# A two-layer hedgehog-attention and gated-MLP kernel whose planner follows a written list of decisions up to the second MLP block

## The chip, the cores and the metric

The kernel runs on one core of a Trainium2 chip. A core has five engines that work side by side, each through its own list of instructions in order: TensorE (PE in the profile, with its weight loads as PEld), VectorE (DVE), ScalarE (ACT), GpSimd (POOL) and SyncE (SP), which here issues nearly all transfers. They wait for each other through semaphores. The metric is device time in microseconds (us): the median of 4 runs was 1060.17 us (1059.71 to 1062.53).

## The reference

```python
def _A_ref(x, wqkv, w_phi, wo):           # S=2048, D=576, H=32 heads of Dh=18
    q, k, v = split of x @ wqkv into heads
    pq, pk = q @ w_phi, k @ w_phi         # per head, 18x18
    phi_q = concat(softmax(pq), softmax(-pq))
    phi_k = concat(softmax(pk), softmax(-pk))
    kv = phi_k^T v;  z = sum of phi_k over the sequence
    return ((phi_q kv) / (phi_q z + 1e-6)) @ wo
def _B_ref(x, w_gate, w_up, w_down):      # F=4608
    return ((x @ w_gate) * (x @ w_up)) @ w_down

x = A_x
x = x + _A_ref(_layernorm(x), A_wqkv, A_w_phi, A_wo)
x = x + _B_ref(_layernorm(x), B_w_gate, B_w_up, B_w_down)
x = x + _A_ref(_layernorm(x), A_wqkv, A_w_phi, A_wo)
x = x + _B_ref(_layernorm(x), B_w_gate, B_w_up, B_w_down)
```

The definitions are shortened here to what is computed. All inputs are bf16; the same weights serve both layers. The input B_x is not used.

## The kernel before

**Stages.** The 2048 rows are 16 tiles of 128, taken in pairs; a pair is also a block of the MLP (8 blocks per layer). All weights but the down weights stay in SBUF. First the raw query and key weights are multiplied by w_phi (threads fusek0 to fusek4 and fuseq0 to fuseq4, t_fuse1: five transposes at L1125, a copy, and two halves of three matmuls each at L1139 with a copy behind each). At the same time TensorE forms Gram products of the raw weights (flag, L999; m2, L981 and L984), from which a bound on the exponents follows. VectorE reduces it to one number in SBUF (L1002, L1008, L1012, with a count on TensorE at L1010), and every engine then loads that number and branches (emit_two, the "mark"). The branch taken here is the fast one, which needs no maxima in the softmax. What stands ahead of the mark in an engine's list runs before the branch.

**Layer 1's attention.** For each pair lnA1 normalises the rows (statistics L1179 to L1193 on VectorE, reciprocal root L1200 and L1202 on ScalarE, product L1212) and puts them in transposed form: by TensorE (L1223) for the first tiles, by a transposing transfer (L1230) for the others. For each tile v1 makes the values and ain1 the keys (both L1256), four exponentials on ScalarE (L1377), one sum on VectorE (L1444), a reciprocal, two multiplications on GpSimd (L1459; on VectorE for tiles 14 and 15); for every second tile TensorE then adds the key-value products of both tiles (L1498). When all are in, VectorE masks the sums (bar1, L1589), and aout1 makes numerators (L1646), a division, a transpose and the output projection of a tile. pq1 projects the queries of tiles 2 to 15 ahead (L1256). The projections are done as two interleaved streams of 64-row matmuls, one in each half of the array; transposes, fused weights, key-value products, numerators and the down projection use its full height.

**The MLP.** For each block gate and up products (glu, gu_quad, L1788, 64-row form, nine groups of four parts) go to hT by ScalarE (L1835) and VectorE (L1837), then dn makes 36 steps of the down product (L1862, L1864) from weights that SP loads slot by slot (wd1, L1763). The attention of later tiles and of layer 2 is woven into the blocks.

**Who sets the order.** Nothing is reordered on the chip. When the program is built, a planner (Sched.run) goes over some hundred threads (generators such as t_ain). Each offers its next step: a group of operations on one engine, one that may go to either of two engines ("alt"), or a transfer. The planner estimates when each could start and records the step with the smallest key

```python
key = (est - self.bias.get(int(th.prio), 0.0) - th.age - th.age0 - (self.hold if late else th.boost), -th.prio)
```

where `age0` comes from the table AGES, by the thread's name. Each engine's list is the order in which its steps were recorded. While no step is far along, `keep_warm` fills TensorE with matmuls on zeros (L957). SP's list is set in the same way: x loads and weight loads from t_load, transposes of xT, eT and oT, and the down weights.

Of the kernel before, what the change touches and what calls it, by code (L numbers as in the profile page):

```python
# [16 lines left out]


AGES = {
    "ain1_0": 64, "ain1_1": -84, "ain1_12": -99, "ain1_13": 49, "ain1_14": 167, "ain1_15": -2, "ain1_2": 26, "ain1_3": 15, "ain1_4": -23,  # L20
    "ain1_5": -128, "ain1_6": -79, "ain1_7": 168, "ain1_8": -58, "ain1_9": -129, "ain2_14": -581, "aout1_0": 4, "aout1_3": -408, "aout2_0": -253,
    "aout2_1": 5, "aout2_2": -160, "aout2_3": -342, "bar1": -1145, "bar2": -651, "bdphi": 663, "bepi0": 843, "bepi6": 1283, "bepi7": -480,
    "flag": -97, "fusek1": 416, "fusek2": 111, "fusek3": 264, "fuseq0": 11, "fuseq4": -53, "init": 108, "k2_6": -644, "k2ln0": 204, "k2ln1": 1008,
    "kv2_6": 13, "kv2_7": -60, "lnA1_0a": 466, "lnA1_0b": 209, "lnA1_1": -113, "lnA1_2": -355, "lnA1_3": 125, "lnA1_6": -93, "lnA1_7": 72,
    "lnB1_0a": 155, "lnB1_0b": -798, "lnB2_0a": -48, "lnB2_0b": 270, "m2": 114, "pq1_11": 129, "pq1_2": -581, "pq1_3": -501, "pq1_4": -398,
    "pq1_7": 408, "pq1_8": 379, "pq1_9": 735, "pq2_11": 158, "pq2_12": -146, "pq2_13": -162, "pq2_14": -2, "pq2_15": -156, "pq2_2": 116, "pq2_3": -76,
    "pq2_5": -209, "pq2_6": -46, "pq2_7": -103, "pq2_8": 448, "pq2_9": 459, "v1_0": -120, "v1_1": 18, "v1_10": -205, "v1_11": 63, "v1_12": -142,
    "v1_13": 263, "v1_2": 195, "v1_3": -176, "v1_4": 267, "v1_5": -60, "v1_6": 31, "v1_7": -90, "v1_8": 232, "v1_9": -307, "v2_14": -73,
    "v2_15": -358,
}  # L30


class Tracker:
# [282 lines left out]
class Sched:  # L316

    def __init__(self, tracker):
        self.tr = tracker
        self.free_at = {e: 800.0 for e in ENGINES}  # L320
        self.busy = {e: 0.0 for e in ENGINES}
        self.threads = []
        self.pools = {}
        self.events = set()
        self.ev_time = {}
        self.dma_free = {e: 0.0 for e in ENGINES}
        self.dma_bw = 280.0
        self.dma_lat = 2000.0
        self.log = []
        self.bias = {}  # L330
        self.pe_mode = 0
        self.fill = None
        self.warm_at = 6000.0
        self.pe_switch = 100.0
        self.lock = None
        self.open = False
        self.hold = -1500.0
        self.port = {"dve": 0.0, "pool": 0.0}
        self.alt_cost = {"dve": 1.0, "pool": 1.0, "act": 1.0}
# [82 lines left out]
    def port_time(self, eng, op, t):  # L422
        if eng == "pool":
            return max(t, self.port["dve"])
        if op.port:
            return max(t, self.port["pool"])
        return t

    def keep_warm(self, limit):

# [24 lines left out]
    def run(self):  # L455
        tr = self.tr
        while True:
            progressed = False
            again = True
            while again:  # L460
                again = False
                for th in list(self.threads):
                    while th.req is not None and th.req[0] not in ("ops", "alt", "pe2", "dma", "acq", "acqn"):
                        r = th.req
# [72 lines left out]
            self.threads = [t for t in self.threads if t.req is not None]  # L537
            if not self.threads:
                break
            best = None  # L540
            pe_est = 1e12
            for th in self.threads:
                r = th.req
                if r[0] == "alt":
                    pick = None
# [28 lines left out]
                    raise RuntimeError("scheduler deadlock: %s" % [(t.name, t.req[:2]) for t in self.threads])  # L574
                continue
            _, th, est = best
            if self.fill is not None:
                self.keep_warm(min(pe_est, est))
            r = th.alt if th.req[0] in ("alt", "pe2") else th.req
            if r[0] == "ops":  # L580
                eng = r[1]
# [108 lines left out]
class K:  # L690
    def __init__(self, nc, A_x, A_wqkv, A_w_phi, A_wo, B_w_gate, B_w_up, B_w_down, out, fast, base=None):
# [13 lines left out]
        self.wtdma = ''  # L705
        self.valt = False
        self.qalt = True
        self.sload = [['raw', 2], ['raw', 1], ['x0', 0], ['raw', 0], ['raw', 3], ['x0', 1], ['x', 1], ['raw', 4], ['x', 2], ['wv', 0], ['x', 3]]
        self.aload = []
        self.fage = 150  # L710
        self.fageq = 0.0
        self.fage2 = 600
        self.lnb = 3
        self.pes = (0, 1, 2, 3, 4, 5, 6, 7, 8, 9, 10, 11, 12, 13)
        self.early = (2, 2)
        self.pex = 2
# [1 line left out]
        self.alt = 1.2  # L718
        self.wage = 10
        self.lnage = -3  # L720
        self.lnlead = 8
        self.pol0 = 1
        self.qdeep = (1, 1)
# [7 lines left out]
        self.qcrit = False  # L731
        self.fq = 3
        self.fqs = 2
        self.fqp = 6.15 if fast else 6.5
        self.sub2pool = False
        self.rboost = 500.0
        self.prio0 = (6, 7)
# [359 lines left out]
    def t_fuse(self, which):  # L1097
# [4 lines left out]
        for kt in range(5):  # L1102
            if which == "q" and not s.fast:
                yield ("wait", ("ain", 1, s.fq + s.fqs * kt))
            yield ("go", s.t_fuse1(which, kt), s.fqp if which == "q" else 8, "fuse%s%d" % (which, kt))
            if which == "q":
                yield ("wait", ("w", which, kt))
        for kt in range(5):
            yield ("wait", ("w", which, kt))
        yield ("sig", ("w", which))  # L1110
# [399 lines left out]
    def t_ain(self, L, st_):  # L1510
# [16 lines left out]
        yield ("wait", ("v", L, st_))  # L1527
        vxs = s.vx_of[(L, st_)]
        if L == 1:
            if s.fast and st_ % 2 == 0:  # L1530
                s.sm_of[st_] = sm
                yield ("sig", ("kf1", st_))
                return
            if s.fast:
                yield ("wait", ("kf1", st_ - 1))
                sm0, vx0 = s.sm_of[st_ - 1], s.vx_of[(1, st_ - 1)]
                for bi in range(2):
                    yield ("ops", "pe", s.kv_ops(sm0, vx0, bi, s.kvb[bi], None, False) + s.kv_ops(sm, vxs, bi, s.kvb[bi], None, False))
                yield ("rel", "smx", sm0 - s.NSM)
                yield ("rel", "vxx", vx0 - s.NVX)  # L1540
                yield ("sig", ("ain", 1, st_ - 1))
            else:
                for bi in range(2):
                    yield ("ops", "pe", s.kv_ops(sm, vxs, bi, s.kvb[bi], None, False))
# [608 lines left out]
```

## Time and profile before

| What | Value |
|---|---|
| median of 4 runs | 1060.17 us |
| the profiled execution's own time | 1060.47 us |
| its span in the profile | 1058.7 us |
| TensorE busy | 1047.1 us (99%) |
| VectorE, ScalarE, GpSimd busy | 480.6, 346.7, 190.7 us |
| first key projection starts | 16.81 us |
| first gate product of block 0 / block 1 starts | 91.93 / 149.57 us |

The span is measured from the first to the last instruction of the profile; the run's time is 1.8 us longer. A timeline line has the start, the length, the engine, the kernel's line, the operation, what it writes and reads, the form and the count; in brackets stands the engine's idle time before it and who ended it. A matmul's form 64*128 uses half the rows of the array. Matmul ends are modelled, so the distance between starts says more than the length. In the table by stage each pair of numbers is an engine's busy time and its count, in the order PE, PEld, DVE, ACT, POOL, then the granted clock, the share of the transfer engines and GB/s.

### The profile page before, as it was taken

The numbers are of one execution on the slowest core, as the hardware profiler recorded it, in microseconds if no ns is written. First come the engines' busy times: TensorE is split into PE (matmuls) and PEld (weight loads), VectorE is DVE, ScalarE is ACT, GpSimd is POOL, SyncE is SP. The second block draws the span as 40 slices with busy tenths as digits, with TensorE's granted clock in tenths as the row PEclk, the third lists the DMA queues.
The fourth block names the chain that finished last, engine by engine and source line by source line (L and its number), as shares of the span: only waits on it lengthen the run. The fifth ranks groups of instructions, "written<-read, shape, count | busy, mean of one in ns | idle before, by whom it ended". The sixth has DMA issues, their size and how long they took to land.

```text
span 1058.7 us, 34326 instructions
## 1 busy us (share of the span) xinstructions
PE 1047.1 (99%) x15789; PEld 803.0 (76%) x15851; DVE 480.6 (45%) x972; ACT 346.7 (33%) x843; POOL 190.7 (18%) x204
## 2 busy tenths in 40 slices
PE   8999999999999999999999999999999999999998
PEld 6778868687786868778695786877778686868685
DVE  7875545264544435444232663534334243424131
ACT  6876314133242414225141742222313131202020
POOL 3952112030221203013110120201010101000000
PEclk9999999999999999999999999999999999999999
DMA  5595281652708164351606034545271918181704
GB/s 163 110 359 143 41 232 39 180 84 83 169 16 228 35 191 73 98 132 37 205 12 202 2 59 145 120 105 156 72 190 41 222 15 239 24 222 19 211 4 149
DMA packets 177625, 127.78 MB, mean 121 GB/s; under 512 B 96576, under 2 KB 175680, under 8 KB 176320
## 3 DMA queue, kind: packets, MB, share of 16 engines
q1 hardware_dynamic: 176864, 125.47, 45.5%
q8 instruction: 126, 2.06, 0.8%
q14 instruction: 27, 0.22, 0.1%
q10 hardware_dynamic: 608, 0.02, 0.0%
HBM read 100.82 MB, written 2.36 MB: 97 GB/s over the span
## 4 chain that ended last, share of the span: by engine, by line
PE 93%; DMA 3%; POOL 2%; DVE 1%; ACT 1%; issue 0%
PE ps L1788 54%; PE ps L1862 20%; PE ps L1256 11%; PE ps L1864 4%; DMA wdr<-in_B_w_down_dram 1%; PE ps L1646 1%; POOL dd_h1g L1459 1%; DMA wdx<-in_B_w_down_dram 1%; PE ps L1498 1%; PE ps L1244 0%; PE ps L1223 0%; POOL xln L1212 0%; POOL dd_w3f L1459 0%; DMA wst<-in_A_w_phi_dram 0%; ACT dd_h1g L1377 0%
## 5 line engine op out<-in xcount | busy, mean ns | idle before, releaser
L1788 PE MATMUL ps<-xT,Wu 64*128 64x256 bf16 x4608 | 581.6, 269 | 0.0
L1788 PE MATMUL ps<-xT,Wg 64*128 64x256 bf16 x4608 | 581.1, 269 | 0.0
L1788 PEld LDWEIGHTS ps<-xT,Wg 64*128 64x128 bf16 x4608 | 430.5, 94 | 30.9 <-issue 3.3
L1788 PEld LDWEIGHTS ps<-xT,Wu 64*128 64x128 bf16 x4608 | 431.7, 94 | 27.9
L1837 DVE TENSOR_TENSOR hT<-ps,hT 128x512 bf16<-128x512 f32 x288 | 199.2, 692 | 302.4 <-ACT hT L1835 302.4
L1835 ACT CAST hT<-ps 128x512 bf16<-128x512 f32 x288 | 168.5, 585 | 400.6 <-PE ps L1788 396.2
L1862 PE MATMUL ps<-wdr,hT 128*128 128x512 bf16 x922 | 238.8, 380 | 0.6 <-DMA wdr<-in_B_w_down_dram 0.3
L1864 PE MATMUL ps<-wdr,hT 128*128 128x64 bf16 x960 | 184.9, 193 | 2.3 <-issue 0.5
L1459 POOL TENSOR_TENSOR dd<-dd,ss 128x576 bf16<-128x576 bf16 x92 | 106.6, 1184 | 441.6 <-ACT ss L1455 441.6
L1862 PEld LDWEIGHTS ps<-wdr,hT 128*128 128x128 bf16 x960 | 93.8, 98 | 111.3 <-DMA wdr<-in_B_w_down_dram 1.8
L1788 PE MATMUL ps<-xT,Wr 64*128 64x256 bf16 x1152 | 165.3, 269 | 0.0
L1212 POOL TENSOR_SCALAR xln<-x_sb,nmean,rstd 128x576 bf16<-128x576 bf16 x56 | 45.4, 821 | 331.4 <-DVE nmean L1193 151.2
L1905 DVE TENSOR_TENSOR x_sb<-ps,x_sb 128x64 bf16<-128x64 f32 x32 | 7.0, 220 | 213.9 <-PE ps L1864 213.9
L1864 PEld LDWEIGHTS ps<-wdr,hT 128*128 128x128 bf16 x960 | 94.1, 98 | 0.2
L1455 ACT ACTIVATE ss<-ss 128x64 f32<-128x64 f32 x92 | 23.8, 259 | 196.2 <-DVE ss L1444 195.3
L1444 DVE TENSOR_REDUCE ss<-dd 128x64 f32<-128x1152 bf16 x48 | 63.8, 1346 | 16.6 <-ACT dd L1377 10.8
L1788 PEld LDWEIGHTS ps<-xT,Wr 64*128 64x128 bf16 x1152 | 63.1, 94 | 6.6
L1862 PE MATMUL ps<-wdx,hT 128*128 128x512 bf16 x168 | 50.4, 380 | 0.6 <-DMA wdx<-in_B_w_down_dram 0.6
L1256 PE MATMUL ps<-Wv,xT 64*128 64x288 bf16 x576 | 49.4, 283 | 0.2 <-ACT dd_h1g L1377 0.2
L1256 PE MATMUL ps<-Wk,xT 64*128 64x288 bf16 x576 | 48.4, 283 | 0.0
L1179 DVE BATCH_NORM_STATS2 st<-x_sb 128x6 f32<-128x288 bf16 x120 | 46.3, 445 | 0.8 <-DVE flag L1012 0.7
L1256 PE MATMUL ps<-Wq,xT 64*128 64x288 bf16 x576 | 40.6, 283 | 0.2
(131 smaller groups left out, 739.1 us busy)
## 6 DMA issues: line engine op xcount, KB each, us to landing
wdr<-in_B_w_down_dram SPq DMA_DIRECT2D x240, 288.0 KB, 3.5
wdx<-in_B_w_down_dram SPq DMA_DIRECT2D x48, 288.0 KB, 3.5
Wg<-in_B_w_gate_dram SPq DMA_DIRECT2D x4, 1152.0 KB, 17.0
Wu<-in_B_w_up_dram SPq DMA_DIRECT2D x4, 1152.0 KB, 18.7
out_dram<-x_sb SPq DMA_DIRECT2D x16, 144.0 KB, 2.7
x_sb<-in_A_x_dram SPq DMA_DIRECT2D x7, 288.0 KB, 3.2
Wraw<-in_A_wqkv_dram SPq DMA_DIRECT2D x5, 304.0 KB, 4.3
xT<-xln SPq DMA_TRANSPOSE x54, 2.5
```

The source lines that it names most:

```text
L1179: ops.append(Op(d_dve(288), (lambda e, j=j, h=h, src=src: e.bn_stats(st[:, sl[j], 6 * h:6 * h + 6], src)), reads=rd, writes=[("st", sl[j], ...
L1212: em = (lambda e, j=j: e.tensor_scalar(xln[:, sl[j], 0:576], x_sb[:, ss[j], :], s.nmean[:, sl[j]:sl[j] + 1], rstd[:, sl[j]:sl[j] + 1], ALU ...
L1256: out.append(Op(61, (lambda e, h=h, k=k, st=(i == 0 and k == 0), sp=(i == 1 and k == 3): e.matmul(s.ps[:, banks[h], 0:N], L[r, k, :], Wm[r ...
L1444: Op(1265, (lambda e: e.tensor_reduce(ss[:, sm, :], e4, AX.X, ALU.add)), reads=s.ddk(sm, 0) + s.ddk(sm, 1), writes=[("ss", sm)]),
L1455: yield ("ops", "act", [Op(200, (lambda e, kw=kw: e.activation(ss[:, sm, :], ss[:, sm, :], **kw)), reads=[("ss", sm)], writes=[("ss", sm)])])
L1459: yield ("alt", [(eng, [Op(dur, (lambda e, ev=ev, rb=rb: e.tensor_tensor(ev, ev, rb, ALU.mult)), reads=s.ddk(sm, br) + [("ss", sm)], write ...
L1498: ops.append(Op(d_pe(CW * n) + 3, (lambda e, k=k, c0=c0, h=h, n=n, st=(first and k == bi): e.matmul(s.ps[:, bank, c0:c0 + CW * n], phi[:, ...
L1788: out.append(Op(54.3, (lambda e, bank=bank, cs=cs, lhsT=lhsT, rhs=rhs, st=st, sp=sp: e.matmul(ps[:, bank, cs].rearrange("p (a n) -> p a n" ...
L1835: yield ("ops", "act", [Op(480, (lambda e, gb=gb, p=p: e.copy(hT[:, p, :], ps[:, gb, :])), reads=[("gu", gb)], writes=[("hT", p)] + (s.raw ...
L1837: yield ("ops", "dve", [Op(600, (lambda e, ub=ub, p=p: e.tensor_tensor(hT[:, p, :], ps[:, ub, :], hT[:, p, :], ALU.mult)), reads=[("gu", u ...
L1862: ops = [Op(d_pe(512), (lambda e: e.matmul(s.ps[:, bank, 0:512], lhsT, s.wslot(slot)[:, fi, 0:512], start=(f == 0), stop=(f == NF - 1))), ...
L1864: Op(d_pe(64) + 3, (lambda e: e.matmul(s.ps[:, z, 64 * sl:64 * sl + 64], lhsT, s.wslot(slot)[:, fi, 512:576], start=(f == 0 and (sl == 0 o ...
```

## The change

The planner gets a list, ORDER, of 980 words. A word is a thread's name, if need be with the engine it should take ("/act"). The n-th time that a name stands there is that thread's n-th step. As long as words are left (`left`), `scripted` takes, among the threads that offer a step now, the one whose step stands earliest in the list; only if none stands there the old key decides. The words reach to the last steps of the down product of block 1 of layer 1 (dn1_1). For a step that may go to two engines the named one is taken, otherwise the cheaper by the old estimate; a word like "/act" behind a step that has no such choice has no effect. Behind the list the planner goes on as before.

Besides: AGES has new numbers for threads that the list covers, and the old ones for all others; the first two raw weight blocks are loaded in the other order; `lnb` goes from 3 to 5 (from which pair on lnA1 waits for the branch); `fqp`, a priority of the fuseq threads, from 6.15 to 6.5; `fqd` and `kvg` are new parameters for the wait between fuseq threads and for which tiles share a group of key-value products.

```diff
@@ -17,17 +17,69 @@
 
 
 AGES = {
...
+ORDER = """
+init side init load init side load load init load init init/act init load/act load flag load/act bdphi fusek1/act m2 fusek1/pool flag/act
+m2/pool lnA1_0a/pool m2 fusek1/pool load fusek2 load/act flag fusek1 lnA1_0a/pool fusek3/pool lnA1_0a lnA1_0b m2 m2 lnA1_0a flag lnA1_0a
+fusek3 fusek3 lnA1_0b/dve lnA1_0b load load lnA1_0b/act lnA1_0a/dve fusek2/pool fusek3 lnA1_0b/act flag load flag fusek0 fusek1 fusek2/dve
+lnA1_0a fusek4 flag fusek0 fusek3 fusek2/pool flag fusek0 lnA1_0b fusek3 fusek2 fusek0/act fusek2 fusek4 fusek4/pool flag fuseq0/act
+init/act fusek1 fusek0 lnA1_0b fusek4/act v1_0 lnA1_1 fuseq0 init fusek4/act fuseq0/pool v1_0/act fusek0 v1_1 fusek4 lnA1_1/dve v1_0 load
+fuseq0/pool lnA1_1 ain1_0 load/pool v1_1 lnA1_1 lnA1_2 lnA1_1 lnA1_1 v1_0/pool ain1_0/act v1_1/act v1_1/act fuseq0/pool ain1_0 fuseq0 lnA1_2
+ain1_0 fuseq1 lnA1_2/dve lnA1_2 lnA1_1 ain1_0/act ain1_0/dve lnA1_1/dve ain1_1/pool lnA1_2 fuseq1 lnA1_1 lnA1_1 ain1_1 ain1_0 lnA1_1 lnA1_3
+ain1_2 lnA1_3 load/dve lnA1_2 fuseq1 ain1_1/dve ain1_1/dve v1_2 ain1_0 ain1_1 ain1_1/dve lnA1_3/pool lnA1_2 fuseq1 lnA1_3/pool ain1_2 ain1_2
+ain1_2 lnA1_2 ain1_1/act v1_2 ain1_0 fuseq1/pool ain1_0 v1_2/dve lnA1_3 ain1_2/pool fuseq1 ain1_2 ain1_3 ain1_1 lnA1_3 v1_3/pool ain1_3/pool
...
+fuseq3 ain1_6 lnA1_5/pool ain1_6 ain1_5 fuseq3 ain1_7 lnA1_4/pool ain1_5/dve v1_6/act fuseq3 v1_7/dve fuseq4 ain1_6/act ain1_7/act ain1_6
+fuseq4 ain1_7/act v1_7/act lnA1_5 ain1_7 ain1_7 ain1_6 v1_7 ain1_7 ain1_8 v1_6/pool fuseq4 v1_8 v1_7 ain1_8 fuseq4 ain1_8/act ain1_5 v1_8
+ain1_8/pool ain1_5 v1_8/pool fuseq4 v1_8 ain1_8 ain1_5 lnA1_6 ain1_9 ain1_6 ain1_7 ain1_7 lnA1_6 ain1_7/pool lnA1_5 ain1_8 fuseq4/dve pq1_2
+lnA1_6 ain1_9/act lnA1_5 lnA1_5 ain1_7 ain1_8 lnA1_6/act ain1_7 lnA1_6 lnA1_7 lnA1_7 lnA1_7/dve lnA1_6 ain1_9 lnA1_6 v1_9 ain1_9 lnA1_6/act
+pq1_2 ain1_8 ain1_8/act lnA1_7 lnA1_7 v1_9 pq1_2 v1_9/act pq1_2 ain1_10/act v1_9 lnA1_6 lnA1_6/dve load load v1_10/dve ain1_10 ain1_9/dve
...
+v1_13 aout1_0 aout1_0 aout1_0 aout1_1 ain1_13 aout1_0 load ain1_12 v1_13 ain1_14/dve v1_13 v1_14 ain1_13 ain1_14 aout1_1 aout1_1 aout1_1
+aout1_1 aout1_0 ain1_14/act ain1_15 ain1_14 ain1_13 v1_14 aout1_1/pool v1_14 ain1_15 v1_14 ain1_15 ain1_11 ain1_14/dve ain1_14 ain1_15/pool
+ain1_15 aout1_0 load aout1_1 ain1_14 ain1_15/pool v1_15 pq1_3 aout1_1 ain1_15/dve v1_15 aout1_0/dve ain1_15 pq1_3 ain1_14 v1_15 pq1_3 pq1_4
+pq1_5/pool pq1_3 aout1_1 ain1_15 v1_15 pq1_4 aout1_0/pool pq1_5 pq1_4/act ain1_15 pq1_6 ain1_14 ain1_11/act pq1_4 pq1_6 pq1_5 pq1_5/act
+pq1_6 pq1_7/pool aout1_0 ain1_13 aout1_0 pq1_6 pq1_7/pool ain1_14/act ain1_15/dve pq1_7 aout1_0 ain1_13/act ain1_15 aout1_0 aout1_1 pq1_7
+wd1/dve wd1 wd1/act pq1_9 bar1 bar1 aout1_1 aout1_2 aout1_0 aout1_1/act aout1_1 aout1_0 aout1_0 pq1_9 aout1_1 pq1_9 pq1_8/act aout1_1
+aout1_2 aout1_0 pq1_9 aout1_0 pq1_10 aout1_1 aout1_1/act aout1_0/pool aout1_0/act aout1_0 aout1_1 aout1_3 aout1_0/pool aout1_1/pool lnB1_0a
+aout1_0 aout1_1 aout1_1 aout1_1/pool lnB1_0a aout1_1/dve aout1_0 lnB1_0b/pool lnB1_0b/dve lnB1_0a aout1_3 lnB1_0b aout1_2 pq1_11 wd1/pool
+wd1 lnB1_0a aout1_1/pool lnB1_0a aout1_1 pq1_11/act pq1_8/pool wd1 aout1_2 lnB1_0a pq1_8 pq1_11/act pq1_11 aout1_2 aout1_3/pool pq1_10/dve
+pq1_12 lnB1_0b aout1_2 pq1_8 pq1_13/act pq1_10 aout1_3 lnB1_0a pq1_12 pq1_12 lnB1_0b pq1_12 aout1_3 pq1_14/pool pq1_13 pq1_14/act pq1_13
+aout1_3 pq1_10 aout1_2 pq1_15 lnB1_0b pq1_15/dve lnB1_0b pq1_14 glu glu glu glu pq1_14/act aout1_3 glu aout1_2 pq1_15 aout1_4 glu glu
+aout1_4 glu glu pq1_13 aout1_4 pq1_15/act glu glu aout1_4/act glu glu glu/pool glu glu/act aout1_4/pool glu glu glu/act glu aout1_4 aout1_2
...
+wd1 dn1_1 aout1_7 dn1_1 aout1_7 dn1_1 wd1 dn1_1 aout1_7 dn1_1 wd1 dn1_1 dn1_1 wd1 dn1_1 dn1_1 wd1 dn1_1 dn1_1 wd1 dn1_1 dn1_1 wd1 dn1_1
+dn1_1 wd1 dn1_1 dn1_1 wd1 dn1_1 dn1_1 wd1 dn1_1 dn1_1 wd1 dn1_1 dn1_1 wd1 dn1_1 dn1_1 wd1 dn1_1 dn1_1 wd1 dn1_1 dn1_1 wd1 dn1_1
+"""
...
 class Tracker:
@@ -329,6 +381,10 @@
         self.log = []
         self.bias = {}
         self.pe_mode = 0
+        self.steps = {}
+        self.seq = []
+        self.rank, self.pick = {}, {}
+        self.script(ORDER.split())
         self.fill = None
         self.warm_at = 6000.0
         self.pe_switch = 100.0
@@ -425,6 +481,54 @@
         if op.port:
             return max(t, self.port["pool"])
         return t
+
+    def script(self, words):
+        n = {}
+        for i, w in enumerate(words):
+            name, _, eng = w.partition("/")
+            k = (name, n.get(name, 0))
+            n[name] = k[1] + 1
+            self.rank[k] = i
+            if eng:
+                self.pick[k] = eng
+        self.left = len(self.rank)
+
+    def scripted(self):
+
+        best = None
+        for th in self.threads:
+            if th.req[0] in ("ops", "alt", "pe2", "dma"):
+                r_ = self.rank.get((th.name, self.steps.get(th.name, 0)))
+                if r_ is not None and (best is None or r_ < best[0]):
+                    best = (r_, th)
+        if best is None:
+            return None
+        th = best[1]
+        r = th.req
+        if r[0] == "alt":
+            pick = None
+            want = self.pick.get((th.name, self.steps.get(th.name, 0)))
+            for i_, (eng, ops) in enumerate(r[1]):
+                e_ = self.port_time(eng, ops[0], max(self.free_at[eng], self.ready(th, i_, eng, ops, False), th.t_ready))
+                f_ = (eng != want) * 1e9 * bool(want) + e_ + sum(o.dur for o in ops) * self.alt_cost[eng]
+                if pick is None or f_ < pick[0]:
+                    pick = (f_, e_, eng, ops)
+            est = pick[1]
+            th.alt = ("ops", pick[2], pick[3])
+        elif r[0] == "pe2":
+            ops = r[1 + self.pe_mode]
+            est = max(self.free_at["pe"], self.ready(th, 10 + self.pe_mode, "pe", ops, True), th.t_ready)
+            th.alt = ("ops", "pe", ops, self.pe_mode)
+        elif r[0] == "ops":
+            eng = r[1]
+            est = self.port_time(eng, r[2][0], max(self.free_at[eng], self.ready(th, 20, eng, r[2], True), th.t_ready))
+            if eng == "pe" and r[2][0].mode != self.pe_mode:
+                est += self.pe_switch
+        else:
+            est = max(self.free_at[r[9] if len(r) > 9 else "sp"], self.ready(th, 21, "sp", r, False), th.t_ready)
+        if self.fill is not None and (r[0] == "pe2" or (r[0] == "ops" and r[1] == "pe")):
+            self.keep_warm(est)
+        return (None, th, est)
     def keep_warm(self, limit):
@@ -537,9 +641,10 @@
             self.threads = [t for t in self.threads if t.req is not None]
             if not self.threads:
                 break
-            best = None
+            best = self.scripted() if self.left > 0 else None
+            told = best is not None
             pe_est = 1e12
-            for th in self.threads:
+            for th in () if told else self.threads:
                 r = th.req
                 if r[0] == "alt":
                     pick = None
@@ -574,8 +679,11 @@
                     raise RuntimeError("scheduler deadlock: %s" % [(t.name, t.req[:2]) for t in self.threads])
                 continue
             _, th, est = best
-            if self.fill is not None:
+            if self.fill is not None and not told:
                 self.keep_warm(min(pe_est, est))
+            self.left -= told
+            self.steps[th.name] = self.steps.get(th.name, 0) + 1
+            self.seq.append((th.name, len(self.log)))
             r = th.alt if th.req[0] in ("alt", "pe2") else th.req
             if r[0] == "ops":
                 eng = r[1]
@@ -705,12 +813,12 @@
         self.wtdma = ''
         self.valt = False
         self.qalt = True
-        self.sload = [['raw', 2], ['raw', 1], ['x0', 0], ['raw', 0], ['raw', 3], ['x0', 1], ['x', 1], ['raw', 4], ['x', 2], ['wv', 0], ['x', 3]]
+        self.sload = [['raw', 1], ['raw', 2], ['x0', 0], ['raw', 0], ['raw', 3], ['x0', 1], ['x', 1], ['raw', 4], ['x', 2], ['wv', 0], ['x', 3]]
         self.aload = []
         self.fage = 150
         self.fageq = 0.0
         self.fage2 = 600
-        self.lnb = 3
+        self.lnb = 5
         self.pes = (0, 1, 2, 3, 4, 5, 6, 7, 8, 9, 10, 11, 12, 13)
         self.early = (2, 2)
         self.pex = 2
@@ -718,6 +826,8 @@
         self.alt = 1.2
         self.wage = 10
         self.lnage = -3
+        self.fqd = 1
+        self.kvg = [0, 2, 4, 6, 8, 10, 12, 14]
         self.lnlead = 8
         self.pol0 = 1
         self.qdeep = (1, 1)
@@ -731,7 +841,7 @@
         self.qcrit = False
         self.fq = 3
         self.fqs = 2
-        self.fqp = 6.15 if fast else 6.5
+        self.fqp = 6.5 if fast else 6.5
         self.sub2pool = False
         self.rboost = 500.0
         self.prio0 = (6, 7)
@@ -1103,8 +1213,8 @@
             if which == "q" and not s.fast:
                 yield ("wait", ("ain", 1, s.fq + s.fqs * kt))
             yield ("go", s.t_fuse1(which, kt), s.fqp if which == "q" else 8, "fuse%s%d" % (which, kt))
-            if which == "q":
-                yield ("wait", ("w", which, kt))
+            if which == "q" and kt >= s.fqd - 1:
+                yield ("wait", ("w", which, kt - s.fqd + 1))
         for kt in range(5):
             yield ("wait", ("w", which, kt))
         yield ("sig", ("w", which))
@@ -1527,18 +1637,22 @@
         yield ("wait", ("v", L, st_))
         vxs = s.vx_of[(L, st_)]
         if L == 1:
-            if s.fast and st_ % 2 == 0:
+            g0 = max(c for c in s.kvg if c <= st_)
+            g1 = min([c for c in s.kvg if c > st_] + [NS]) - 1
+            if s.fast:
                 s.sm_of[st_] = sm
+            if s.fast and st_ < g1:
                 yield ("sig", ("kf1", st_))
                 return
             if s.fast:
-                yield ("wait", ("kf1", st_ - 1))
-                sm0, vx0 = s.sm_of[st_ - 1], s.vx_of[(1, st_ - 1)]
+                for t_ in range(g0, g1):
+                    yield ("wait", ("kf1", t_))
                 for bi in range(2):
-                    yield ("ops", "pe", s.kv_ops(sm0, vx0, bi, s.kvb[bi], None, False) + s.kv_ops(sm, vxs, bi, s.kvb[bi], None, False))
-                yield ("rel", "smx", sm0 - s.NSM)
-                yield ("rel", "vxx", vx0 - s.NVX)
-                yield ("sig", ("ain", 1, st_ - 1))
+                    yield ("ops", "pe", [o for t_ in range(g0, g1 + 1) for o in s.kv_ops(s.sm_of[t_], s.vx_of[(1, t_)], bi, s.kvb[bi], None, False)])
+                for t_ in range(g0, g1):
+                    yield ("rel", "smx", s.sm_of[t_] - s.NSM)
+                    yield ("rel", "vxx", s.vx_of[(1, t_)] - s.NVX)
+                    yield ("sig", ("ain", 1, t_))
             else:
                 for bi in range(2):
                     yield ("ops", "pe", s.kv_ops(sm, vxs, bi, s.kvb[bi], None, False))
```

## Prediction before the run

> **What bounds the kernel now.** I read the page first: busy times, then the chain that ended last.
>
> ```profile
> PE 1047.1 (99%) x15789; PEld 803.0 (76%) x15851; DVE 480.6 (45%) x972; ACT 346.7 (33%) x843; POOL 190.7 (18%) x204
> ...
> PE 93%; DMA 3%; POOL 2%; DVE 1%; ACT 1%; issue 0%
> ```
>
> TensorE is the bound; a new order only helps where TensorE stands still or pays for being asked in a bad sequence. The table by stage, for the stretch that the list rewrites, says how little standing still there is (first pair of numbers: length, then TensorE's busy time).
>
> ```profile
> 0.00:13.20 13.20, 10.32 (x132) 8.84 (x132) 7.94 (x29) 6.37 (x15) 3.99 (x17) 1.00 0.81 260
> 13.20:25.00 11.80, 11.78 (x164) 7.97 (x166) 11.27 (x30) 9.79 (x32) 4.75 (x8) 1.00 0.19 58
> 25.00:47.00 22.00, 21.58 (x338) 15.41 (x336) 19.23 (x37) 18.55 (x68) 21.57 (x21) 1.00 0.59 116
> 47.00:75.00 28.00, 27.86 (x451) 20.89 (x450) 20.85 (x28) 21.33 (x71) 20.90 (x20) 1.00 0.90 291
> 75.00:92.00 17.00, 17.00 (x236) 12.27 (x234) 10.92 (x26) 12.98 (x35) 3.39 (x3) 1.00 0.90 311
> ```
>
> Idle: 2.88 us before 13.2, 0.58 us from there to 92, where the first gate/up product starts. But "busy" contains modelled ends, so I also took the spacing of matmul starts in the timeline. First the branch on the flag:
>
> ```profile
> 10.53 0.89 DVE L1002 TENSOR_REDUCE cst<-ps 128x1 f32<-128x384 f32 x2
> ...
> 11.18 0.82 POOL L1212 TENSOR_SCALAR xln<-x_sb,nmean,rstd 128x576 bf16<-128x576 bf16 x1 [7.27 <-DVE cst L1002]
> ...
> 11.46 0.57 DVE L1008 TENSOR_SCALAR f<-cst 128x2 bf16<-128x2 f32 x1
> ...
> 12.08 0.19 PE L1010 MATMUL ps<-one,f 128*1 128x1 bf16 x2 [0.61 <-DVE f L1008]
> 12.33 0.14 DVE L1012 TENSOR_SCALAR flag<-ps 1x1 int32<-1x1 f32 x1
> ...
> 13.20 0.57 PE L1223 MATMUL ps<-ident,xln 128*128 128x128 bf16 x6 [0.93 <-DVE flag L1012]
> 13.60 0.31 PE L1139 MATMUL ps<-BDphi,WTk 128*64 128x144 bf16 x3
> ```
>
> TensorE waits 0.61 us for the comparison and 0.93 us for flag and branch: 1.54 us with nothing queued ahead of the branch. Second, the price of changing between the 64-row matmuls (two halves of the array side by side) and full-height ones:
>
> ```profile
> 17.43 0.65 PE L1256 MATMUL ps<-Wv,xT 64*128 64x288 bf16 x8
> 17.92 0.65 PE L1256 MATMUL ps<-Wk,xT 64*128 64x288 bf16 x8
> 18.50 0.32 PE L1139 MATMUL ps<-BDphi,WTq 128*128 128x108 bf16 x3
> 18.65 0.56 PE L1223 MATMUL ps<-ident,xln 128*128 128x128 bf16 x6
> ...
> 21.36 0.32 PE L1139 MATMUL ps<-BDphi,WTq 128*128 128x144 bf16 x3
> 21.61 0.79 PE L1256 MATMUL ps<-Wk,xT 64*128 64x288 bf16 x10
> ```
>
> Eight 64-row matmuls before more of the same take 17.92 - 17.43 = 0.49 us, before full-height ones 18.50 - 17.92 = 0.58; three full-height ones 0.15 before their like, 0.25 before 64-row ones. A switch costs 0.09 to 0.10 us each way, 0.19 us there and back. Third, waits inside the stretch; the largest is this one:
>
> ```profile
> 45.49 0.33 PE L1139 MATMUL ps<-BDphi,WTq 128*64 128x108 bf16 x3
> 45.76 0.35 PE L1498 MATMUL ps<-vx_h2g,dd_h1g 128*128 128x76 bf16 x5
> 46.34 0.69 PE L1498 MATMUL ps<-vx_h2g,dd_h1g 128*128 128x76 bf16 x13 [0.23 <-POOL dd_h1g L1459]
> ```
>
> Here the spacing reaches 0.43 us where 0.04 is normal: 0.39 lost. Going through all starts from 13.2 to 92 the same way (against 0.12 us for a pair of 64-row matmuls), the other losses are 0.19 at 24.65, 0.25 at 28.6, 0.17 at 28.9, 0.09 at 40.4, 0.08 at 50.5, 0.17 at 53.5, 0.19 at 58.1, 0.2 at 71.3, 0.16 at 82.1 and about 0.2 in crumbs: 2.1 us with the first. So what an order can win is about 1.5 + 2.1 us, plus switches.
>
> **The change, part by part.** *Edits that move nothing by themselves.* The pair list for the key-value products is the old pairing, and the depth of 1 for the fused query weights gives the old wait. The ages that changed all belong to threads that the list steers; those of later threads are as before. The layer norms of pairs 3 and 4 no longer wait for the branch, but the list puts their first step behind the flag's last. Raw weight blocks 1 and 2 swap places in the load queue: equal sizes (304 KB), so the landings (3.68 and 4.72 us) swap owners. Together 0; a cost needs a reader of block 2 standing first, and the list asks for block 1 first.
>
> *The start.* I laid the list's TensorE words before the flag's ninth and last step beside the timeline. Before: five weight transposes, seven of the ten key-weight halves, one layer norm transpose. New: the same five, eight halves, both layer norm transposes, most of the extra behind the matmul that counts the flag. What moves into the idle time is one transpose group (13.60 - 13.20 = 0.40 us) and one half (13.84 - 13.60 = 0.24): 0.64 us. Does the flag come later? The last Gram block can't start before its weights land (9.38; it ran at 9.89), so it can gain at most 0.5. Behind it stand the maxima (0.89), the comparison, the count, the flag; the list puts copies of about 0.45 us each (rows of the same copies at 9 to 12 us) between them, two probably on VectorE. Against that, the comparison took 0.57 us beside GpSimd's 0.82 us normalisation, and a VectorE operation of that size elsewhere 0.15 (its negated mean, 9.95). The Trainium skill (SBUF — State Buffer, Who interferes with whom) says that VectorE in its two-port modes and GpSimd hold a shared pair of ports exclusively for a whole instruction; the row agrees in kind (11.46 + 0.57 = 12.03, GpSimd's end 12.00). The list doesn't fix which engine normalises the second tile: on VectorE the 0.4 us goes. By row and rule the flag moves by -0.5 to +0.5; I take 0. Cost also: the negative one, that the weight check's first reduction now follows the 0.9 us product of mask and weights on VectorE, so its matmul stands some 0.4 us at 5.6; the Gram block that ends the chain is bound by its landing, which hides it. Sum **-0.65** (-1.2 to +0.3).
>
> *Switches.* Counting changes of form up to the last down product of block 1: 58 in the trace of before, 60 in the list. One pair more: **+0.19**. The Trainium skill (TensorEngine Tiling (Array Packing), Key Properties) says that a change of tiling mode drains the engine, and TensorE: Matmul & The Clock Gate, Single matmul latency, puts a drain near 175 ns. By that rule a pair would be 0.35 us; the measured rows give half of it, and I use them. This rule speaks against the change: nothing was won on switches.
>
> *Waits from 13.2 to 92.* The list keeps the shape: first key-value products behind tile 4, those of tiles 4 and 5 behind tile 8. GpSimd's queue ahead of the products of tiles 6 and 7 is the same 8 normalisations and 16 multiplications: 8 x 0.81 + 16 x 1.165 = 25.1 us from its start at 20.67, plus an idle 0.85, which ends at 46.3 to 46.6, the wait shown. In the list 0.6 us more TensorE work (half a query projection) stands ahead of that wait, and the ScalarE steps before GpSimd's first normalisation (its reciprocal root) follow the first key projection, which the start brings 0.6 us forward. The two roughly keep step, so this wait shrinks but stays possible. Tiles 14 and 15 get more cover: 12 half projections between the last key projection and its product (9.4 us by 0.56 each plus transposes and products), where before 6.6 us sufficed. New exposure: the second tile's transpose before block 0 is followed by only 8 matmuls (0.49 us) before the gate product reads its copy (0.49 us on VectorE, 0.69 on ScalarE, some 0.1 around): +0.15 (0 to +0.4). Of the 2.1 us I let half go, with no row that says which half: -1.1 (-2.1 to +1.0, since a new order can make as many). Sum **-0.95**.
>
> *Transfers.* The load of x pair 3 moves behind the branch on SP: issued near 13.1 it lands about 2.9 us later (as pair 4 did, 13.10 to 15.99); its first reader was at 21.9. The gate and up weights keep their place behind the last normalised tile's transposes; the last one landed at 84.40 for a reader at 91.9, so 7.5 us of slip are free. Behind six down-weight loads stand the attention transposes of tiles 2 and 3 (landed 91.5 and 97.4, read at 103.8). The output projection of tile 2 comes earlier: 8.1 us behind its numerator (4.5 + 0.5 + 56 x 0.0545), where the chain took 8.0 (103.8 to the landing at 111.81); its transpose took 4.4 us with two others near, the next 2.6, and the list issues those others later. **0** (to +0.4).
>
> *After block 1* the planner is the old one with the old ages: **0**, bounded by 1 us each way, since the few waits there depend on how the first blocks leave the queues.
>
> Sum: -0.65 + 0.19 - 0.95 = -1.4 us. Against the profiled execution's 1060.47 (span 1058.7, 1.8 around it) that is 1059.1; the median 1060.17 lies 0.3 lower, so **1058.8**.
>
> **The rivals.** *Small gain* (0.44): the sum; 1057.8 to 1062.2 is within 0.2%, 2.1 us, about what a measurement of this kernel can tell from no change. This holds too if the order does nothing: GpSimd's chain at 46 us then swallows the gain of the start, 1060.0. *Nearly all of it goes* (0.34): 1.5 at the flag and most of the 2.1, less 0.19, so about -3: 1057.2. For it: every wait named is short and has other work near; against: GpSimd's row at 25 to 47 is 98% busy, and that chain is not shortened. *Slower* (0.22): GpSimd's chain starts late. TensorE is in order, and everything queued behind the products of tiles 6 and 7 waits with them. By my sum TensorE gets there at about 45.4, so a start after 20.3 costs us for us; from 23.8 on (2.1 + 1.4 later) the kernel is measurably slower, at 24.5 it takes 1063. Before, GpSimd idled 6.5 us for exactly this start, on ScalarE's root behind a full queue; against it, the list keeps the root behind the same four exponentials.
>
> **Numbers.** Faster 0.36 (the second case and the edge of the first), within 0.2% 0.42, slower 0.22. Range 1056.4 (all waits and the flag, -3.8) to 1062.4 (GpSimd's late start and one more wait); the small gain alone: 1057.8 to 1060.4.
>
> **What would show it.** Right: TensorE has work between count and branch, the first key projection starts near 16.2 (16.81 now), gate/up starts at 90.5 (91.93) and everything from there is shifted evenly. Wrong: the flag's operation on VectorE after 12.6, GpSimd's first long run later than 20.7, a gap before the first gate product above 0.4, or spacing lost after 210 us.

## The result, and the profile after

The changed kernel takes 1059.12 us (median of 34 runs, 1057.6 to 1062.27) where the kernel before, run beside it, takes 1060.5 (55 runs, 1058.77 to 1063.45). The ratio is 0.9988, with a 95% interval of 0.9983 to 0.9994: 0.6 to 1.8 us faster, 1.3 in the middle. The forecast was 1058.8, 1.4 us below the runs of before, and "within 0.2%" as the likeliest class; both held. How the 1.3 us came about did not follow the forecast. The profiled execution took 1059.69 us (span 1057.9), 0.78 less than that of before.

The page first: busy times, then the chain that ended last.

```profile
PE 1047.6 (99%) x15791; PEld 805.7 (76%) x15853; DVE 480.0 (45%) x971; ACT 346.1 (33%) x836; POOL 193.8 (18%) x208
...
PE 96%; DMA 1%; DVE 1%; ACT 1%; issue 0%; POOL 0%
```

TensorE is the bound as before. The table by stage (length, then busy time and count of TensorE, and so on as before) answers to the five rows of the prediction:

```profile
0.00:13.20 13.20, 12.01 (x152) 10.73 (x154) 7.67 (x29) 8.20 (x18) 4.64 (x20) 1.00 0.74 238
13.20:25.00 11.80, 11.59 (x165) 8.32 (x167) 11.02 (x29) 9.85 (x34) 5.99 (x8) 1.00 0.42 103
25.00:47.00 22.00, 21.70 (x340) 15.44 (x336) 19.83 (x39) 16.72 (x59) 21.81 (x22) 1.00 0.57 102
47.00:75.00 28.00, 27.64 (x447) 20.81 (x443) 21.78 (x27) 21.99 (x71) 20.83 (x19) 1.00 0.97 293
75.00:92.00 17.00, 16.85 (x233) 12.14 (x234) 11.56 (x29) 11.34 (x30) 4.83 (x5) 1.00 0.74 294
```

Up to 13.2 us TensorE is idle for 1.19 us instead of 2.88: 1.69 less. From there to 92 us it is idle for 1.02 us instead of 0.58: 0.44 more. So the start earned, and the list behind it gave something back. VectorE's timeline at the check of the weights, and TensorE's in the same stretch, show the start:

```profile
10.09 0.89 DVE L1112 TENSOR_REDUCE cst<-ps 128x1 f32<-128x384 f32 x2 [0.55 <-PE ps L1109]
11.02 0.23 DVE L1118 TENSOR_SCALAR f<-cst 128x2 bf16<-128x2 f32 x1
...
11.55 0.14 DVE L1122 TENSOR_SCALAR flag<-ps 1x1 int32<-1x1 f32 x1
12.40 0.49 DVE L1336 COPY xT<-ps 128x640 bf16<-128x640 bf16 x1 [0.71 <-PE ps L1249]
```

```profile
8.87 0.56 PE L1333 MATMUL ps<-ident,xln 128*128 128x128 bf16 x6
9.43 0.73 PE L1109 MATMUL ps<-Wraw 128*128 128x128 bf16 x10
10.00 0.44 PE L1235 MATMUL ps<-ident,Wraw 128*128 128x128 bf16 x5
...
11.30 0.19 PE L1120 MATMUL ps<-one,f 128*1 128x1 bf16 x2
11.42 0.32 PE L1249 MATMUL ps<-BDphi,WTk 128*128 128x144 bf16 x3
11.59 0.56 PE L1333 MATMUL ps<-ident,xln 128*128 128x128 bf16 x6
12.08 0.58 PE L1249 MATMUL ps<-BDphi,WTk 128*128 128x108 bf16 x6
...
15.46 0.41 PE L1366 MATMUL ps<-Wk,xT 64*128 64x288 bf16 x3
```

TensorE no longer stands still behind the count (11.30): the second tile's transpose (11.59, 13.20 before) and two more groups run while the flag is made and read. But the chain to the flag is shorter too. The last Gram group starts at 9.43 (9.89 before) although its weights land at 9.38 in both, the comparison takes 0.23 us (0.57 before), and the flag is done at 11.69 instead of 12.47. The first key projection starts at 15.46 (16.81), the first gate product at 91.45 (91.93), block 1 at 148.92 (149.50 by the first gate product in the trace of before; the 149.57 in the table further up is 0.07 too late). Of a lead of 1.35 us at the first key projection 0.48 reaches block 0, and the span ends 0.7 earlier. The waits on TensorE that stand out between the two are these:

```profile
18.20 0.57 PE L1333 MATMUL ps<-ident,xln 128*128 128x128 bf16 x6 [0.15 <-ACT Wq L1254]
26.91 0.78 PE L1366 MATMUL ps<-Wk,xT 64*128 64x288 bf16 x9 [0.24 <-ACT dd_h1g L1487]
60.70 0.66 PE L1366 MATMUL ps<-Wq,xT 64*128 64x288 bf16 x8 [0.30 <-PE ps L1366]
```

In spacing of starts they cost 0.3, 0.4 and 0.47 us. The wait on GpSimd at 46 us, the largest of before, is gone: the same 18 products now run as one row.

```profile
45.69 0.86 PE L1608 MATMUL ps<-vx_h2g,dd_h1g 128*128 128x76 bf16 x18
```

### The profile page after: what moved, and what is told of

Its sections match the earlier page's. It is cut to its first block, busy times and chain, and to the rows that moved or that the text cites. A ratio compares the mean times of both kernels' runs of the same rounds, so it can differ in the third digit from the quotient of the medians.

```text
span 1057.9 us, 34326 instructions
## 1 busy us (share of the span) xinstructions
PE 1047.6 (99%) x15791; PEld 805.7 (76%) x15853; DVE 480.0 (45%) x971; ACT 346.1 (33%) x836; POOL 193.8 (18%) x208
## 4 chain that ended last, share of the span: by engine, by line
PE 96%; DMA 1%; DVE 1%; ACT 1%; issue 0%; POOL 0%
PE ps L1902 53%; PE ps L1976 22%; PE ps L1366 13%; PE ps L1978 4%; PE ps L1760 1%; PE ps L1608 1%; DMA wdr<-in_B_w_down_dram 0%; PE ps L1354 0%; PE ps L1333 0%; DMA xT<-xln 0%; DVE dd_h1g L1569 0%; DMA wdx<-in_B_w_down_dram 0%; PE ps L1109 0%; PE ps L1249 0%; PE ps L1067 0%
```

## The experiments

**How they are read.** The order of a list is fixed when the program is built, so two kernels with the same list behind the branch can be laid on each other instruction by instruction: the lead of one over the other then shows where it is won or lost. Two things disturb it. The last of the five raw weight loads lands between 9.22 and 9.99 us in the six traces, with no pattern in the orders (9.38 and 9.86 with the old start; 9.38, 9.58, 9.99 and 9.22 with the new one). With the new start the last Gram group follows this landing in three of four traces; with the old start it stands further back in TensorE's list and does not (below). So where I take the difference of the landings off a lead, the result is good to about 0.1 us and not better. And medians of eleven or twelve runs have intervals of about a whole us either way. All four kernels shared their 35 runs of the kernel before (median 1061.16).

**New start, old order behind the branch.** The first 73 decisions are those of the changed kernel; the rest is the old kernel's own sequence, read from its planner and written as words, with the old ages, `lnb` and `fqp`.

```diff
-        self.lnb = 5
+        self.lnb = 3
...
-        self.fqp = 6.5 if fast else 6.5
+        self.fqp = 6.15 if fast else 6.5
...
 flag fusek0 lnA1_0b fusek3/act fusek2 fusek0/act fusek2/act fusek4/dve fusek4 flag/dve
-fuseq0 init/pool fusek1/act fusek0 lnA1_0b/dve fusek4/act v1_0 lnA1_1/dve fuseq0/dve
+load fusek1/act init/pool lnA1_1/dve lnA1_0b/act load init/pool fuseq0 v1_0 fusek4/act fuseq0/dve
...
```

> The new order up to the end of the input check (its first 73 decisions, with the swapped weight loads), and the old order from the branch on. Theory 'the start earns, the list behind it gives a part back': the first key projection starts near 15.5 us (16.81 before, 15.46 in the changed kernel), the lead of 1.3 is kept or nearly kept through the old order, the first gate/up product starts at 90.6 to 91.0 (91.93 before, 91.45 in the changed kernel), and the whole is 0.9 to 1.3 us under the kernel before and 0.2 to 0.5 under the changed one. Rival 'the new list behind the branch earns as much as it was forecast to': the old list loses the lead in its own waits on VectorE and GpSimd, the gate starts at 91.7 or later, and the time is within 0.4 us of the kernel before.

Measured: 1059.73 us (11 runs, 1058.74 to 1061.7), ratio to the kernel before 0.9985 (0.9974 to 0.9996), so 0.4 to 2.8 us faster. The interval leaves out "no change": the start alone is worth something. That it beats the changed kernel by 0.2 to 0.5, as expected, cannot be told from the ratios (0.9985 and 0.9988). The places in the trace were missed: the first key projection stands at 16.28 (15.5 was expected) and the gate at 91.44 (90.6 to 91.0). The reason is a wait at the seam, which neither theory foresaw. TensorE's timeline of this kernel, then ScalarE's:

```profile
11.78 0.56 PE L1345 MATMUL ps<-ident,xln 128*128 128x128 bf16 x6
...
13.17 0.29 PE L1378 MATMUL ps<-Wv,xT 64*128 64x288 bf16 x1
13.69 0.78 PE L1378 MATMUL ps<-Wv,xT 64*128 64x288 bf16 x9 [0.23 <-ACT Wk L1266]
```

```profile
11.27 1.76 ACT L1266 CAST Wk<-ps 128x288 bf16<-128x288 f32 x4
13.24 0.40 ACT L1266 CAST Wk<-ps 128x288 bf16<-128x288 f32 x1 [0.21 <-DVE st L1301]
```

The first value projection needs a PSUM bank that ScalarE empties with a cast at 13.24, after four casts of the same kind and the branch. The old order puts this projection ahead of a weight half, which was right when TensorE got there at 14.22. The lead of this kernel over the kernel before, for the same TensorE instruction:

```
second tile's transpose   -1.42
next weight half          -1.08
value projection, 13.69   -0.54
up to 60 us               -0.54  (unchanged over some 690 matmuls)
60 to 144 us              -0.49
down products, 145.47     -0.75
down products, 146.46     -0.28
```

So half of the lead that stood at the weight half is lost in one wait; after that the old list keeps it, to within 0.05 us, up to 144 us. Near the end of block 0 a down weight that lands late takes another 0.47 (TensorE's timeline again; the kernel before loses 0.26 of its own just ahead of it, hence the -0.75):

```profile
145.67 0.19 PE L1990 MATMUL ps<-wdr,hT 128*128 128x64 bf16 x1
146.18 0.39 PE L1988 MATMUL ps<-wdr,hT 128*128 128x512 bf16 x1 [0.31 <-DMA wdr<-in_B_w_down_dram]
```

**Old start, new order behind the branch.** The mirror image: the old kernel's 71 decisions and its load order, then the new list.

```diff
-        self.sload = [['raw', 1], ['raw', 2], ['x0', 0], ...
+        self.sload = [['raw', 2], ['raw', 1], ['x0', 0], ...
...
-fusek0 lnA1_0b fusek3/act fusek2 fusek0/act fusek2/act fusek4/dve fusek4 flag/dve
+lnA1_0b/pool fusek2/act fusek2 flag fusek4/dve flag/dve lnA1_0b fusek0/act fusek2/act fusek4
 fuseq0 init/pool ...
```

> The old order up to the end of the input check (71 decisions, old order of the weight loads), and the new order from the branch on. Theory 'the start earns, the list behind it gives a part back': the first key projection starts near 16.8 us, the waits of 2.9 us between 13 and 92 stay, the first gate/up product starts at 92.4 to 92.8, and the time is 0.5 to 0.9 us above the kernel before. Rival 'the new list earns': the gate starts at 91.0 to 91.5 in spite of the late start, and the time is 0.4 to 0.9 below the kernel before.

Measured: 1061.39 us (11 runs, 1059.6 to 1063.02), ratio 1.0002 (0.9992 to 1.0012), so between 0.8 faster and 1.3 slower than before; by itself that interval does not exclude a small gain by the list. The trace tells more. The first key projection stands at 17.21, the gate at 92.84, beyond the 91.0 to 91.5 of the rival. From the second tile's transpose (13.54) to the gate it takes 79.30 us; the kernel before takes 78.73 for the same stretch (13.20 to 91.93). So with the old start the new list is 0.57 us slower up to block 0 (0.13 of it between 13.95 and 15.85, where the two orders meet). With the new start the same comparison gives 79.43 (the third experiment, 12.19 to 91.62) and 79.39 (the changed kernel, 79.86 less the 0.47 at 60.70, a wait that the other kernels with this list do not have) against 79.12 for the old list (79.66 less the 0.54 at the seam): 0.27 to 0.31 slower. The list behind the branch costs 0.3 to 0.6 us, if the wait at the seam is not put down to the old list. As the two ran, with that wait in it, the old list behind the new start was 0.23 to 0.27 us slower than the new one; whether it has an order without that wait was not tried.

Laid on the changed kernel, which has the same list, this trace also gives the worth of the start a second time. The changed kernel leads by 1.96 at the second tile's transpose, 1.62 at the weight half behind it and 1.75 at 15.85 us, and this stays (1.75 to 1.79) until 61.95, where its own wait of 0.47 comes.

VectorE's and GpSimd's timelines of this kernel repeat what the check of the weights looked like before:

```profile
10.88 0.89 DVE L1123 TENSOR_REDUCE cst<-ps 128x1 f32<-128x384 f32 x2
11.80 0.57 DVE L1129 TENSOR_SCALAR f<-cst 128x2 bf16<-128x2 f32 x1
...
12.68 0.13 DVE L1133 TENSOR_SCALAR flag<-ps 1x1 int32<-1x1 f32 x1
```

```profile
11.53 0.82 POOL L1333 TENSOR_SCALAR xln<-x_sb,nmean,rstd 128x576 bf16<-128x576 bf16 x1 [7.61 <-DVE cst L1123]
```

**The list cut off at block 0.** Of the 980 words the first 580 stay; then the planner decides with the new ages.

```diff
-... fusek2 flag (the 400 words from block 0 to the last down product of block 1)
+"""
```

> The written order is cut off where block 0 begins; from there on the planner decides with the new ages. Theory 'all of the gain lies ahead of block 0': the same as the changed kernel, within 0.4 us on either side, the first gate product at 91.4 to 91.5. Rival 'the written order of blocks 0 and 1 is worth something of its own': the start of block 1 (148.9 in the changed kernel) comes 0.5 us or more later, and the whole is slower by as much.

Measured: 1059.83 us (12 runs, 1058.46 to 1062.77), ratio 0.9987 (0.9974 to 1.0000). That is the changed kernel's ratio within 0.0001. From the first gate product of block 0 to that of block 1 it takes 57.64 us (91.62 to 149.26), the changed kernel 57.47, the kernel before 57.57. The words for blocks 0 and 1 are worth at most 0.2 us, and the rival's 0.5 is not there. As in the first experiment a down weight is late near 146 us (0.32 by spacing). Here too the start can be weighed: against the old start with the same list this kernel leads by 1.01 at the weight half and 1.15 at 15.85, 1.21 from 75 us on.

**Three repairs in the list.** In the changed kernel three waits were aimed at: the second tile's transpose before block 0 and its copy go ahead by two projections' halves, a query projection's second half goes between the halves of its neighbour, and a weight cast goes to VectorE.

```diff
-... pq1_11 pq1_11 pq1_8 ... pq1_12 pq1_14 pq1_13 pq1_14 pq1_15 lnB1_0b pq1_15 glu ...
+... pq1_11 pq1_8 pq1_11 ... pq1_12 pq1_14 lnB1_0b pq1_13 pq1_14 glu ... glu pq1_15 pq1_15 glu ...
...
-fuseq0/act
+fuseq0/dve
```

(The order in which TensorE got them, not the words as written: the last projection, pq1_15, was not meant to move.)

> The changed kernel with three moves: the second tile's output transposes before the first gate product (and their copy) six TensorE groups earlier, one query projection's first half between the two halves of its neighbour, and one weight cast on VectorE in place of ScalarE. Theory: what ends the waits of 0.3 at 18.20, 0.25 at 84.08 and 0.23 at 91.45 is the late copy, the second half directly behind the first, and the late cast, so these three go and nothing takes their place: the first gate product starts at 90.7 to 91.0 (91.45 in the changed kernel), and the whole is 0.4 to 0.7 us under the changed kernel. Rival 'a wait removed there is taken up by the next one, since the engine that is late stays late': the gate starts at 91.3 or later and the time is within 0.2 of the changed kernel.

Measured: 1060.62 us (11 runs, 1059.95 to 1062.83), ratio 0.9994 (0.9983 to 1.0004); the profiled run took 1060.41, 0.72 more than that of the changed kernel, where 0.4 to 0.7 less was expected. The theory falls in two of three places. The wait at 18.20 is still there, with another operation of ScalarE in the cast's place, which is what the rival said:

```profile
18.48 0.57 PE L1344 MATMUL ps<-ident,xln 128*128 128x128 bf16 x6 [0.17 <-ACT dd_h1g L1498]
```

Another 0.2 to 0.3 went at 24.07, on ScalarE's exponentials too. The exchange of halves at 84 us brought some 0.25, and 0.16 of it went at 85.24, on GpSimd. The third place can't be judged: with the transpose ahead of it the last query projection no longer got its PSUM banks in time, and the planner recorded it behind 25 gate and up steps of block 0. That is why the gate appears at 90.30 (18 matmuls, 1.1 us, are missing ahead of it) and block 1 at 150.09, 1.17 later than in the changed kernel. Inside block 0 the projection waits 0.6 us for a bank that VectorE empties:

```profile
118.32 0.28 PE L1377 MATMUL ps<-Wq,xT 64*128 64x288 bf16 x1
119.19 1.51 PE L1377 MATMUL ps<-Wq,xT 64*128 64x288 bf16 x17 [0.59 <-DVE x_sb L1848]
```

**Not tried.** The new start with the old list and without the wait at the seam, which by an estimate from the sums below (-1.2 for the start, nothing for the list) would reach block 0 some 0.3 to 0.6 us ahead of the changed kernel; the changed kernel with the second tile's transpose and a weight half put back behind the branch, which would weigh the filled idle time by itself; and the changed kernel with GpSimd's normalisation laid over the comparison. These runs were not made.

## Why the prediction was right, and where it was not

The sum was -0.65 + 0.19 - 0.95 = -1.4 us. The runs give -1.3, but not by this sum: the start earned about half a us more than forecast, and the waits brought at best half of theirs, by the likelier reading nothing. That the whole came out so close is luck. The signs named beforehand say so too: the first key projection came at 15.46 (16.2 forecast), the first gate product at 91.45 (90.5).

**The start: -0.65 forecast, about -1.2 found.** Two pieces make it up: how much earlier the flag is made, and how much of the idle time behind it is filled. The step that failed is "By row and rule the flag moves by -0.5 to +0.5; I take 0." From the landing of the last raw weights to the end of the flag it took 3.09 and 2.95 us with the old start, 2.31, 2.30 and 2.30 with the new one (2.73 in the fourth experiment, where the weights land at 9.22 and the first tile's transpose keeps TensorE until 9.70): the flag itself moved by 0.65 to 0.78. Two things make this up, and both stood in the prediction's lower bound:

- The comparison. 0.57 us in both kernels with the old start, 0.23 in all four with the new one: -0.34. With the old start GpSimd normalises at that moment, and the comparison ends 0.03 us after GpSimd does, in both traces (12.03 after 12.00, 12.38 after 12.35). With the new start GpSimd does nothing then; its timeline in the changed kernel:

```profile
7.90 0.82 POOL L1322 TENSOR_SCALAR xln<-x_sb,nmean,rstd 128x576 bf16<-128x576 bf16 x1 [3.98 <-DVE st L1289]
12.38 0.23 POOL L1059 TENSOR_SCALAR_AFFINE_SELECT maskf<-maskf 128x20 bf16<-128x20 bf16 x1 [3.65 <-DVE flag L1122]
```

  The same is seen far from the start, where the lists play no part. In the trace of before 21 negated means of two columns (128x2) take 0.16 us and the one that meets GpSimd takes 0.31, ending 0.03 us after it (VectorE's timeline, then GpSimd's):

```profile
157.95 0.31 DVE L1193 TENSOR_SCALAR nmean<-mv 128x2 f32<-128x2 f32 x1
```

```profile
155.91 2.33 POOL L1459 TENSOR_TENSOR dd<-dd,ss 128x576 bf16<-128x576 bf16 x2
```

  Copies of 128x64 within SBUF (L1671) take 0.18 us alone, 0.59 and 0.31 beside GpSimd, and end 0.04 us after it. Not every operation waits: the negated mean of one column (128x1) takes 0.15 us in the middle of a GpSimd multiplication too (81.67), and the reductions and reads of PSUM keep their lengths. This agrees with the Trainium skill (SBUF — State Buffer, Who interferes with whom): VectorE in its two-port modes and GpSimd exclude each other from a shared pair of ports for a whole instruction. The profile does not show the mode. The prediction had the rule and the 0.4 us, but left the engine open ("The list doesn't fix which engine normalises the second tile") and set copies on VectorE against it. No copy more than before came: one stands between comparison and flag, at 11.15 as at 11.93 before. The new start normalises the first tile on GpSimd early (7.90) and the second on VectorE (9.11). No experiment moved this overlap by itself; the two starts, the coinciding ends and the other places speak for it.
- The last Gram group. The prediction took its start at 9.89, 0.5 us behind the landing, and allowed "at most 0.5". It was not waiting for data then: the old order puts ten weight transposes and a half ahead of it. TensorE's timeline before:

```profile
9.17 0.73 PE L1125 MATMUL ps<-ident,Wraw 128*128 128x128 bf16 x10
9.74 0.31 PE L1139 MATMUL ps<-BDphi,WTk 128*128 128x144 bf16 x3
9.89 0.72 PE L999 MATMUL ps<-Wraw 128*128 128x128 bf16 x10
```

  The new order puts transposes of that kind behind it, so that in three of four traces it starts 0.05 us after its weights land (0.51 and 0.37 with the old start), and they fill TensorE while VectorE reduces: -0.32 to -0.46.

The other piece, filling the idle time between count and branch (0.64 forecast), can be read without the landings: from the end of the flag to the weight half behind the second tile's transpose (13.60 before, 12.33 in the changed kernel) it takes 1.13 us in both traces with the old start and 0.64 in all four with the new one, 0.5 less. This step held. Together that is 1.15 to 1.28. Three pairs of traces with the same list weigh the whole as a check: at that weight half the new start leads by 1.08 (kernel before and first experiment), 1.62 (second experiment and changed kernel) and 1.01 (second and third), or 1.28, 1.14 and 1.14 with the differences of the landings taken off.

**Switches: +0.19.** The changed trace has 60 changes of form up to the last down product of block 1 and the one of before 58, as counted. The price was not measured again by itself; it is part of the next term.

**Waits from 13.2 to 92: -0.95 forecast, +0.1 to +0.4 found.** The list costs 0.3 to 0.6 up to block 0; less 0.19 for the switches, that is what its waits add. Even if the wait at the seam is put down to the old list, the new one's waits save 0.4 to 0.5, half of what was forecast. The step that failed is "Of the 2.1 us I let half go, with no row that says which half." Some did go: GpSimd's first long run starts at 19.66 (20.67 before, and not later than 20.7 as the prediction asked), and the wait at 46 us is gone. New ones came at the same rate. Before, GpSimd had the longest wait; now ScalarE is what TensorE stands for at 18.20 and 26.91. That a new order makes as many waits as it removes was written beside the number as its upper bound, and half of a total without an owner was taken all the same. The exposure of the second tile's copy before the gate was +0.15 forecast and 0.23 found (90.21 transpose, 90.86 to 91.35 copy, gate at 91.45).

**Transfers: 0.** The late load of x (issued 12.32, landed 15.10) made nobody wait, and neither did the gate and up weights (the last landed at 84.47). Not counted: down weights that land late near the end of block 0. All six traces lose something to them between 142 and 149 us (0.26 before, 0.17 in the changed kernel, 0.47 and 0.32 in the first and third experiment), with no order by lead.

**After block 1: 0.** The first gate product of block 1 to the end of the span takes 909.0 us, 909.2 before. Held.

**The whole.** The start's -1.2 and the list's +0.3 to +0.6 leave -0.6 to -0.9 at block 0. The two profiled executions, with equal landings, are 0.48 apart there and took 0.78 less in the end, with a wait of 0.47 at 60.70 in that of after. The cause of that wait stays open: the three other kernels with the same list do not show it. The medians say -1.3 (-0.6 to -1.8), a range that takes in the sum and the 0.78.

Of the rivals, "nearly all of it goes" came nearest at the flag (1.5 forecast, about 1.2 found) and failed on the waits. "Slower" needed GpSimd's chain later than 20.3; it came a us earlier than before.

## What to carry to other kernels

A decision that gates all engines is worth taking apart instruction by instruction: what stands ahead of its inputs on an in-order engine, and what runs on the other engine at that moment, were worth more here than filling the idle time behind it. A saving should be written down only against a wait that has an owner and a reason to go; "half of the rest" is a guess, and a new order brings as many small waits as it removes. Two kernels that share a list and differ only ahead of it can be laid on each other instruction by instruction, and this places a gain within about 0.1 us where medians could only place it within a us.

## What the runs showed of the hardware

- With loads of the same sizes ahead of it the fifth raw weight load of a start-up burst (304 KB, issued at 4.1) landed between 9.22 and 9.99 us in six traces. At the start of a kernel of 1060 us this is as large as most of the effects looked for.
- A lead that had settled by 16 us stayed the same to within 0.06 us for 45 to 57 us and some 700 to 850 matmuls: the waits in these lists come at the same instructions again, whether the whole is 0.5 or 1.7 us early or late (the wait at 60.70 in one trace apart).
- A short VectorE operation can last until a GpSimd instruction of 0.8 to 1.2 us beside it ends (0.57 in place of 0.23 us, 0.31 in place of 0.16, 0.59 in place of 0.18). Others of the same engine (one column, reductions, reads of PSUM) kept their lengths beside GpSimd.
